# Scores and the state's output part on 64-row halves of the TensorE array, the new state on 64-column halves

## The chip, the cores and the metric

The kernel runs on one core of a Trainium2 chip. The metric is the device time of one execution in microseconds (us); less is better. Three runs of the kernel before the change took 210.63, 210.71 and 213.97 us, with a median of 210.71 us.

Times below are in us unless marked ns. TensorE is shown as two rows in the profile: PE is the stream of matmuls, PEld the stream of weight loads (each matmul multiplies a moving operand with a stationary one, which its weight load has put into the 128x128 array). DVE is VectorE, ACT is ScalarE, POOL is GpSimd, and SP issues most of the transfers.

## The reference

Two parts are computed one after the other: a gated linear attention (4 batches, 8 heads, 768 steps, head size 48), and a two-layer feed-forward over its output (3072 tokens, 384 to 2048 to 384).

```python
f = 1.0 / (1.0 + np.exp(-f_logit))
for t in range(S):
    state = f[:, :, t, :, None] * state + np.einsum('bhd,bhe->bhde', k[:, :, t], v[:, :, t])
    y[:, :, t] = np.einsum('bhd,bhde->bhe', q[:, :, t], state)
...
h = x @ w_in
g = np.maximum(0.01 * h, h)
return (g @ w_out).astype(np.float32)
```

The state of one head is a 48x48 matrix. Inputs and output are float32.

## The kernel before

**Units.** The 768 steps of a batch are cut into 6 chunks of 128 steps. A unit is one chunk of one batch with its 8 heads, and there are 24 units, ordered by chunk first and batch second (units 0 to 3 are chunk 0 of the four batches). All work of a unit is done on tiles with 128 steps or 128 channels on the partitions, in bf16 with float32 sums.

**Within a unit.** `gate_act` and `gate_pe` turn the gate's logits into logarithms and sum them over the steps with a triangular matrix (`cs`, L117, and its totals per channel, L120). `decay_act` makes the decay factors with the exponential. `scale_pool` multiplies k and q with them on POOL into `kh` and `qh`. These have 64 columns for each head, 48 of them used and the rest zero, so that a pair of heads fills 128 columns. `turn_pe` transposes the four pairs of `kh` and `qh` (L149): now a pair of heads stands on 128 partitions, the first head on partitions 0 to 63, the second on 64 to 127. `turn_dve` copies the result from PSUM to SBUF: `kT` in one copy (L155), and q in two copies (L157, L158) into the block-diagonal tile `qbd`, which has a 128-column block for each head of the pair, with zeros where the other head's partitions are.

`score_pe` then takes `kT` of a pair as the stationary operand and the two blocks of `qbd` as the moving one: one matmul with 256 columns gives the scores of both heads (L168, 4 matmuls in a unit, two PSUM banks `pw`, each with two pairs). `mask_dve` multiplies each bank with the triangle (L175). `mix_pe` gathers the unit's output `py` in one bank: the state's part with `qbd` as the stationary operand and the old state as the moving one (L187, 8 matmuls with 48 columns, not in chunk 0), and the part within the chunk with the masked scores (L191, 8 matmuls with 48 columns). `y_act` copies `py` to SBUF (L226, 384 elements on each partition). `state_pe` forms the new part of the state for a pair of heads in one matmul with 96 columns (L203, 4 matmuls, not in the last chunk); of its 128x96 result only the two diagonal blocks are used, and `state_dve` adds them with one instruction for each half of the partitions (L213, L214). `state_pool` applies the decay and makes the bf16 copy of the state (L221, L222). `x_pe` and `x_dve` transpose the output for the feed-forward.

**The feed-forward of a unit.** `up` does a quarter of the first layer (12 matmuls with 128 columns, L250, then one activation, L252), `down` half of the second (8 matmuls with 384 columns, L259), `put` copies the result out of PSUM (L264) and stores it.

**Order.** The schedule is written out by hand, and each engine works through its instructions in the order of the program. Iteration i of the main loop does the feed-forward of unit i and, between its parts, the attention of unit i+1 and the gates of units i+2 and i+3. On TensorE the order in an iteration is: transposes (`turn_pe`), two `up`, scores, gate sums, two `up`, `mix_pe`, `state_pe`, half of `down`, `x_pe`, half of `down`.

**PSUM.** Pool `ps_w` has two banks and holds only the scores. Pool `ps_s` has two banks with the tag "sm" and holds `cs`, `py`, `pt` and `px` in turn. The feed-forward's `pm` has two banks, its output one, the transposes one.

Of the kernel before, what the change touches and what calls it, by code (L numbers as in the profile page):

```python
# [9 lines left out]
FP32 = mybir.dt.float32  # L10
BF16 = mybir.dt.bfloat16
# [4 lines left out]
def kernel(  # L16
# [10 lines left out]
    nc = tc.nc  # L27

    B, H, S, D = q.shape
# [3 lines left out]
    P2 = H // 2  # L33
    KD, FF = moe_w_in.shape
# [6 lines left out]
    const = ctx.enter_context(tc.tile_pool(name="const", bufs=1))  # L41
    inp = ctx.enter_context(tc.tile_pool(name="inp", bufs=6))
    work = ctx.enter_context(tc.tile_pool(name="work", bufs=3))
# [6 lines left out]
    ps_w = ctx.enter_context(tc.tile_pool(name="ps_w", bufs=2, space=bass.MemoryType.PSUM))  # L50
    ps_s = ctx.enter_context(tc.tile_pool(name="ps_s", bufs=2, space=bass.MemoryType.PSUM))
# [5 lines left out]
    ut = const.tile([128, 128], BF16, tag="ut")  # L57
# [10 lines left out]
    lfs = [const.tile([128, H, 64], BF16, name=f"lf{i}", tag=f"lf{i}") for i in range(3)]  # L68
    qhs = [const.tile([128, H, 64], BF16, name=f"qh{i}", tag=f"qh{i}") for i in range(3)]
    khs = [const.tile([128, H, 64], BF16, name=f"kh{i}", tag=f"kh{i}") for i in range(3)]  # L70
    qbds = [const.tile([128, P2, 2, 128], BF16, name=f"qbd{i}", tag=f"qbd{i}") for i in range(2)]
    state_f = [const.tile([128, P2, D], FP32, name=f"sf{b}", tag=f"sf{b}") for b in range(B)]
    state_b = [const.tile([128, P2, D], BF16, name=f"sb{b}", tag=f"sb{b}") for b in range(B)]
    for t in lfs + qhs + khs + qbds:
        nc.vector.memset(t, 0.0)
    for t in state_f:
        nc.vector.memset(t, 0.0)
# [25 lines left out]
    st = {}  # L103
# [48 lines left out]
    def turn_dve(u):  # L152
        tp = st[u].pop("tp")
        kT = work.tile([128, P2, 128], BF16, name="kT", tag="kT")
        nc.vector.tensor_copy(out=kT, in_=tp[:, 0])  # L155
        qbd = qbds[u % 2]
        nc.vector.tensor_copy(out=qbd[0:64, :, 0, :], in_=tp[0:64, 1])  # L157
        nc.vector.tensor_copy(out=qbd[64:128, :, 1, :], in_=tp[64:128, 1])  # L158
        st[u]["kT"] = kT

    def score_pe(u):
        kT, qbd = st[u].pop("kT"), qbds[u % 2]
        st[u]["pw"] = []
        for g in range(2):
            pw = ps_w.tile([128, 4, 128], FP32, name="pw", tag="pw")
            for i in range(2):
                p = 2 * g + i
                nc.tensor.matmul(pw[:, 2 * i:2 * i + 2, :], kT[:, p, :], qbd[:, p, :, :], start=True, stop=True)  # L168
            st[u]["pw"].append(pw)

    def mask_dve(u):
        st[u]["wm"] = []
        for pw in st[u].pop("pw"):
            wm = work.tile([128, 4, 128], BF16, name="wm", tag="wm", bufs=6)
            nc.vector.tensor_mul(wm, pw, ut[:, None, :].to_broadcast([128, 4, 128]))  # L175
            st[u]["wm"].append(wm)

    def mix_pe(u):
        c, b = units[u]
        s = st[u]  # L180
        qbd, v_b, wms = qbds[u % 2], s["v"], s.pop("wm")
        py = ps_s.tile([128, 512], FP32, name="py", tag="sm")
        n = H if c == 0 else 2 * H
        i = 0
        if c > 0:
            for h in range(H):
                nc.tensor.matmul(py[:, h * D:(h + 1) * D], qbd[:, h // 2, h % 2, :], state_b[b][:, h // 2, :],  # L187
                                 start=(i == 0), stop=(i == n - 1))
                i += 1
        for h in range(H):  # L190
            nc.tensor.matmul(py[:, h * D:(h + 1) * D], wms[h // 4][:, h % 4, :], v_b[:, h, :],  # L191
                             start=(i == 0), stop=(i == n - 1))
            i += 1
        s["py"] = py

    def state_pe(u):
        c, b = units[u]
        if c == NCH - 1:
            return
        kh, v_b = khs[u % 3], st[u]["v"]  # L200
        pt = ps_s.tile([128, P2, 2 * D], FP32, name="pt", tag="sm")
        for p in range(P2):
            nc.tensor.matmul(pt[:, p, :], kh[:, 2 * p:2 * p + 2, :], v_b[:, 2 * p:2 * p + 2, :],  # L203
                             start=True, stop=True)
        st[u]["pt"] = pt

    def state_dve(u):
        c, b = units[u]
        if c == NCH - 1:
            return  # L210
        pt = st[u].pop("pt")
        sf = state_f[b]
        nc.vector.tensor_add(sf[0:64], sf[0:64], pt[0:64, :, 0:D])  # L213
        nc.vector.tensor_add(sf[64:128], sf[64:128], pt[64:128, :, D:2 * D])  # L214

    def state_pool(u):
        c, b = units[u]
# [5 lines left out]

    def y_act(u):
        xn = work.tile([128, KD], BF16, name="xn", tag="xn")
        nc.scalar.copy(out=xn, in_=st[u].pop("py")[:, 0:KD])  # L226
        st[u]["xn"] = xn

    def x_pe(u):
# [57 lines left out]
    gate_act(2)  # L287
    turn_pe(0)
    turn_dve(0)
    score_pe(0)  # L290
    mask_dve(0)
    mix_pe(0)
    state_pe(0)
    y_act(0)
    state_dve(0)
    state_pool(0)
    x_pe(0)
    x_dve(0)

    for i in range(NU):  # L300
# [3 lines left out]
        if n1 < NU:  # L304
            turn_pe(n1)
            turn_dve(n1)
        up(i, 0)
        up(i, 1)
        if n1 < NU:
            score_pe(n1)  # L310
            mask_dve(n1)
# [6 lines left out]
        if n1 < NU:  # L318
            mix_pe(n1)
            y_act(n1)  # L320
            state_pe(n1)
            state_dve(n1)
            state_pool(n1)
# [38 lines left out]
```

## Time and profile before

| what | value |
|---|---|
| median of three runs | 210.71 us |
| span of the profiled execution | 209.4 us |
| PE busy | 177.8 us (85%), 2432 matmuls |
| PEld busy | 146.1 us (70%), 2432 weight loads |
| ACT busy | 108.7 us (52%) |
| DVE busy | 97.4 us (46%) |
| POOL busy | 76.8 us (37%) |
| granted TensorE clock | 1.000 |

The span runs from the first instruction to the last; the profile lists no other time for this execution, so its own time is taken as the span and the 1.3 us by which the median stands above it. A group of the profile has a line number, an engine, what is written from what, the shape, and the mean duration of one instruction. For a matmul the group also names the part of the array it runs on; before the change this is 128*128 everywhere. A matmul's duration holds its way through the array, which overlaps with the next matmuls, so the pace of a row of matmuls is read from their starts and not from their durations.

From 41.69 us on the main loop is regular. An iteration takes 7.10 us where the next unit is in chunk 0, and 7.30 us from chunk 1 on (63.20 to 70.50, 128.92 to 136.22 and others). In an iteration of 7.30 us DVE is busy for 3.99 us, ACT for 4.47 us and POOL for 3.09 us, while PE has no gap that the profile shows.

### The profile page before, as it was taken

Reading aid. Unit: us, or ns where it says so; the run is one execution under the profiler, and the core shown is the slowest. Engines: PE = TensorE matmul, PEld = TensorE weight load, DVE = VectorE, ACT = ScalarE, POOL = GpSimd, SP = SyncE. Lnnn points to the kernel's source line nnn. Section 1 sums busy time; section 2 is a strip of 40 time slices with the busy share of each in tenths; the row PEclk is TensorE's granted clock in tenths of the full one; section 3 lists DMA queues with packets and bytes.
Section 4 is the critical chain, followed back from the end, with each engine's and each line's share of the span. In section 5 each row is a group of like instructions: output and inputs, shape, how many; then the busy total and the mean of one; then the engine's idle time right before and its main releaser. Section 6 shows DMA issues by size and latency. Waiting matters only on the chain.

```text
span 209.4 us, 5831 instructions
## 1 busy us (share of the span) xinstructions
PE 177.8 (85%) x2432; PEld 146.1 (70%) x2432; DVE 97.4 (46%) x223; ACT 108.7 (52%) x237; POOL 76.8 (37%) x129
## 2 busy tenths in 40 slices
PE   0000149999999999999999999999999999999993
PEld 0000028788779788877988887798888778877881
DVE  8000044466546545654654565465455545633511
ACT  4000332775576458447645845774585567555540
POOL 8300071542553255145325524532552454034000
PEclk9999999999999999999999999999999999999999
DMA  6999999998796479568647846956695681100111
GB/s 114 171 195 184 199 191 189 156 219 163 121 176 143 105 136 177 114 118 163 147 102 133 186 111 116 157 116 141 128 187 113 119 153 41 38 28 18 38 41 38
DMA packets 106267, 27.12 MB, mean 130 GB/s; under 512 B 100352, under 2 KB 105472, under 8 KB 106240
## 3 DMA queue, kind: packets, MB, share of 16 engines
q1 hardware_dynamic: 103296, 23.60, 59.5%
q0 software_dynamic: 2944, 3.15, 9.0%
q8 instruction: 19, 0.31, 0.6%
q14 instruction: 8, 0.07, 0.1%
HBM read 25.17 MB, written 4.72 MB: 143 GB/s over the span
## 4 chain that ended last, share of the span: by engine, by line
PE 83%; issue 10%; POOL 4%; DVE 1%; ACT 0%; POOLq 0%
PE pm L250 32%; PE pm L259 30%; PE pw L168 6%; PE tp L149 5%; PE py L191 2%; PE px L233 2%; PE py L187 2%; PE cs L117 2%; PE pt L203 2%; POOL w_in_b L94 2%; POOL w_out_b L99 1%; POOL kh L139 1%; PE cs L120 1%; DVE wm L175 1%; POOL qh L140 1%
## 5 line engine op out<-in xcount | busy, mean ns | idle before, releaser
L252 ACT ACTIVATE gT<-pm 128x512 bf16<-128x512 f32 x96 | 56.2, 601 | 64.1 <-PE pm L250 62.3
L250 PE MATMUL pm<-xT,w_in_b 128*128 128x128 bf16 x1152 | 73.4, 221 | 0.0
L259 PE MATMUL pm<-w_out_b,gT 128*128 128x384 bf16 x384 | 70.1, 326 | 0.0
L250 PEld LDWEIGHTS <-w_in_b 128*128 128x128 bf16 x1152 | 67.2, 99 | 0.6
L139 POOL TENSOR_TENSOR kh<-k_raw,em_t 128x384 bf16<-128x384 f32 x24 | 22.0, 916 | 110.5 <-ACT em_t L129 105.7
L259 PEld LDWEIGHTS <-gT 128*128 128x128 bf16 x384 | 35.2, 98 | 18.8
L175 DVE TENSOR_TENSOR wm<-pw,ut 128x512 bf16<-128x512 f32 x48 | 30.9, 686 | 12.7 <-PE pw L168 11.9
L117 PE MATMUL cs<-lf,ut 128*128 128x384 bf16 x24 | 8.1, 339 | 24.9 <-ACT lf L111 24.9
L264 DVE COPY osb<-pm 128x384 f32<-128x384 f32 x24 | 13.4, 558 | 26.6 <-PE pm L259 26.6
L109 ACT ACTIVATE e_t<-f_raw 128x384 f32<-128x384 f32 x24 | 12.9, 536 | 23.7 <-DMA f_raw<-in_f_logit_dram 23.7
L120 PEld LDWEIGHTS <-lf 128*128 128x128 bf16 x80 | 5.0, 99 | 25.2 <-issue 23.8
L140 POOL TENSOR_TENSOR qh<-q_raw,a_t 128x384 bf16<-128x384 f32 x24 | 21.9, 914 | 0.0
L155 DVE COPY kT<-tp 128x512 bf16<-128x512 bf16 x24 | 10.0, 415 | 23.6 <-PE tp L149 23.6
L238 DVE COPY xT<-px 128x384 bf16<-128x384 bf16 x24 | 8.6, 358 | 22.2 <-PE px L233 22.2
L213 DVE TENSOR_TENSOR sf<-sf,pt 64x192 f32<-64x192 f32 x20 | 6.9, 346 | 22.2 <-PE pt L203 22.2
L168 PE MATMUL pw<-qbd,kT 128*128 128x256 bf16 x96 | 14.8, 277 | 1.3 <-DVE qbd L158 1.3
L129 ACT ACTIVATE em_t<-cs 128x384 bf16<-128x384 f32 x24 | 11.8, 491 | 4.5 <-PE cs L120 3.7
L111 ACT ACTIVATE lf<-e_t 128x384 bf16<-128x384 f32 x24 | 12.5, 523 | 0.8
L168 PEld LDWEIGHTS <-kT 128*128 128x128 bf16 x96 | 9.4, 99 | 4.3 <-DVE kT L155 0.8
L226 ACT CAST xn<-py 128x384 bf16<-128x384 f32 x24 | 11.4, 474 | 1.5 <-PE py L191 1.5
L142 POOL CAST v_b<-v_raw 128x384 bf16<-128x384 f32 x24 | 12.1, 505 | 0.0
L130 ACT ACTIVATE a_t<-cs 128x384 bf16<-128x384 f32 x24 | 11.6, 485 | 0.0
(37 smaller groups left out, 155.3 us busy)
## 6 DMA issues: line engine op xcount, KB each, us to landing
f_raw<-in_f_logit_dram SPq DMA_DIRECT2D x24, 192.0 KB, 3.2
k_raw<-in_k_dram SPq DMA_DIRECT2D x24, 192.0 KB, 3.8
q_raw<-in_q_dram SPq DMA_DIRECT2D x24, 192.0 KB, 4.0
v_raw<-in_v_dram SPq DMA_DIRECT2D x24, 192.0 KB, 4.3
out_dram<-osb SPq DMA_DIRECT2D x24, 192.0 KB, 2.0
w_in_b<-in_moe_w_in_dram POOLq DMA_DIRECT2D x6, 256.0 KB, 8.8
w_out_b<-in_moe_w_out_dram POOLq DMA_DIRECT2D x2, 768.0 KB, 18.2
```

The lines of the kernel that those rows point to most:

```text
L109: nc.scalar.activation(e, f, AF.Exp, scale=-1.0)
L111: nc.scalar.activation(lf[:, :, 0:D], e, AF.Ln, bias=1.0)
L117: nc.tensor.matmul(cs[:, 0:H * D], ut, lf[:, :, 0:D], start=True, stop=True)
L139: nc.gpsimd.tensor_mul(khs[u % 3][:, :, 0:D], r["k"], st[u]["em"])
L140: nc.gpsimd.tensor_mul(qhs[u % 3][:, :, 0:D], r["q"], st[u]["a"])
L142: nc.gpsimd.tensor_copy(out=v_b, in_=r["v"])
L168: nc.tensor.matmul(pw[:, 2 * i:2 * i + 2, :], kT[:, p, :], qbd[:, p, :, :], start=True, stop=True)
L175: nc.vector.tensor_mul(wm, pw, ut[:, None, :].to_broadcast([128, 4, 128]))
L250: nc.tensor.matmul(pm[:, i, :], w_in_b[:, kk, ff * 128:(ff + 1) * 128], s["xT"][:, kk, :], start=(kk == 0), stop=(kk == NK - 1))
L252: nc.scalar.activation(s["g"][:, 4 * g:4 * g + 4, :], pm, AF.Prelu, alpha=0.01)
L259: nc.tensor.matmul(s["pm2"], s["g"][:, ff, :], w_out_b[:, ff, :], start=(ff == 0), stop=(ff == NF - 1))
L264: nc.vector.tensor_copy(out=osb, in_=st[u]["pm2"])
```

## The change

The block-diagonal `qbd` goes. q is copied from PSUM in one piece into `qT`, in the same layout as `kT`. A score matmul now takes one head: 48 partitions of one half (0 to 47 or 64 to 111), so that it uses 64 rows of the array and 128 columns, with 128 moving columns; the two heads of a pair are issued one after the other, on the two row halves, and write to different banks. The state's part of y is split over row halves in the same way, its 8 matmuls keeping 48 moving columns. Heads of even number gather in one PSUM bank and those of odd number in another; the two output tiles `py` now come from pool `ps_w`, whose two banks they share in turn with the scores. `y_act` becomes two copies of 192 elements with a strided output. The new state is made one head at a time: 128 rows and 64 columns of the array, 48 moving columns, 8 matmuls where there were 4, and the result lies compactly, so that one addition replaces two.

```diff
-    qbds = [const.tile([128, P2, 2, 128], BF16, name=f"qbd{i}", tag=f"qbd{i}") for i in range(2)]
...
-    for t in lfs + qhs + khs + qbds:
+    for t in lfs + qhs + khs:
         nc.vector.memset(t, 0.0)
...
         nc.vector.tensor_copy(out=kT, in_=tp[:, 0])
-        qbd = qbds[u % 2]
-        nc.vector.tensor_copy(out=qbd[0:64, :, 0, :], in_=tp[0:64, 1])
-        nc.vector.tensor_copy(out=qbd[64:128, :, 1, :], in_=tp[64:128, 1])
-        st[u]["kT"] = kT
+        qT = work.tile([128, P2, 128], BF16, name="qT", tag="qT")
+        nc.vector.tensor_copy(out=qT, in_=tp[:, 1])
+        st[u]["kT"], st[u]["qT"] = kT, qT
 
     def score_pe(u):
-        kT, qbd = st[u].pop("kT"), qbds[u % 2]
-        st[u]["pw"] = []
-        for g in range(2):
-            pw = ps_w.tile([128, 4, 128], FP32, name="pw", tag="pw")
-            for i in range(2):
-                p = 2 * g + i
-                nc.tensor.matmul(pw[:, 2 * i:2 * i + 2, :], kT[:, p, :], qbd[:, p, :, :], start=True, stop=True)
-            st[u]["pw"].append(pw)
+        kT, qT = st[u].pop("kT"), st[u]["qT"]
+        pws = [ps_w.tile([128, P2, 128], FP32, name="pw", tag="pw") for j in range(2)]
+        for p in range(P2):
+            for j in range(2):
+                rows = slice(64 * j, 64 * j + D)
+                nc.tensor.matmul(pws[j][:, p, :], kT[rows, p, :], qT[rows, p, :], start=True, stop=True)
+        st[u]["pw"] = pws
...
     def mix_pe(u):
         c, b = units[u]
         s = st[u]
-        qbd, v_b, wms = qbds[u % 2], s["v"], s.pop("wm")
-        py = ps_s.tile([128, 512], FP32, name="py", tag="sm")
-        n = H if c == 0 else 2 * H
-        i = 0
+        qT, v_b, wms = s.pop("qT"), s["v"], s.pop("wm")
+        pys = [ps_w.tile([128, P2, D], FP32, name="py", tag="pw") for j in range(2)]
         if c > 0:
-            for h in range(H):
-                nc.tensor.matmul(py[:, h * D:(h + 1) * D], qbd[:, h // 2, h % 2, :], state_b[b][:, h // 2, :],
-                                 start=(i == 0), stop=(i == n - 1))
-                i += 1
-        for h in range(H):
-            nc.tensor.matmul(py[:, h * D:(h + 1) * D], wms[h // 4][:, h % 4, :], v_b[:, h, :],
-                             start=(i == 0), stop=(i == n - 1))
-            i += 1
-        s["py"] = py
+            for p in range(P2):
+                for j in range(2):
+                    rows = slice(64 * j, 64 * j + D)
+                    nc.tensor.matmul(pys[j][:, p, :], qT[rows, p, :], state_b[b][rows, p, :],
+                                     start=(p == 0), stop=False)
+        for j in range(2):
+            for p in range(P2):
+                nc.tensor.matmul(pys[j][:, p, :], wms[j][:, p, :], v_b[:, 2 * p + j, :],
+                                 start=(c == 0 and p == 0), stop=(p == P2 - 1))
+        s["py"] = pys
 
     def state_pe(u):
...
-        pt = ps_s.tile([128, P2, 2 * D], FP32, name="pt", tag="sm")
+        pt = ps_s.tile([128, P2, D], FP32, name="pt", tag="sm")
         for p in range(P2):
-            nc.tensor.matmul(pt[:, p, :], kh[:, 2 * p:2 * p + 2, :], v_b[:, 2 * p:2 * p + 2, :],
-                             start=True, stop=True)
+            for j in range(2):
+                nc.tensor.matmul(pt[64 * j:64 * j + 64, p, :], kh[:, 2 * p + j, :], v_b[:, 2 * p + j, :],
+                                 start=True, stop=True)
...
-        nc.vector.tensor_add(sf[0:64], sf[0:64], pt[0:64, :, 0:D])
-        nc.vector.tensor_add(sf[64:128], sf[64:128], pt[64:128, :, D:2 * D])
+        nc.vector.tensor_add(sf, sf, pt)
...
     def y_act(u):
         xn = work.tile([128, KD], BF16, name="xn", tag="xn")
-        nc.scalar.copy(out=xn, in_=st[u].pop("py")[:, 0:KD])
+        xv = xn.rearrange("t (p j d) -> t j p d", p=P2, j=2)
+        for j, py in enumerate(st[u].pop("py")):
+            nc.scalar.copy(out=xv[:, j], in_=py)
```

`mask_dve` keeps its two instructions of 128x512 in shape; a bank now holds four heads of the same parity.

More of the change, by code (lines that the diff above doesn't have):

```diff
@@ L173, in mask_dve @@
         for pw in st[u].pop("pw"):
-            wm = work.tile([128, 4, 128], BF16, name="wm", tag="wm", bufs=6)
-            nc.vector.tensor_mul(wm, pw, ut[:, None, :].to_broadcast([128, 4, 128]))
+            wm = work.tile([128, P2, 128], BF16, name="wm", tag="wm", bufs=6)
+            nc.vector.tensor_mul(wm, pw, ut[:, None, :].to_broadcast([128, P2, 128]))
             st[u]["wm"].append(wm)
```

## Prediction

> **What bounds the kernel now.** I read the page's busy shares first, then the chain that ended last, then that chain piece by piece through one iteration, then the instructions in order of time around the pieces that change.
>
> ```profile
> PE 177.8 (85%) x2432; PEld 146.1 (70%) x2432; DVE 97.4 (46%) x223; ACT 108.7 (52%) x237; POOL 76.8 (37%) x129
> PE 83%; issue 10%; POOL 4%; DVE 1%; ACT 0%; POOLq 0%
> ```
>
> TensorE holds 83% of the chain, and no other engine is busy for much over half of the span. So an edit counts by the TensorE time it takes or gives in an iteration; DVE, ACT and POOL count only if they come too late for TensorE. One iteration of the chain (start, duration, piece):
>
> ```profile
> 128.92 0.45 PE tp L149 x8
> 129.37 1.34 PE pm L250 x24
> 130.71 0.57 PE pw L168 x4
> 131.28 0.16 PE cs L117
> 131.44 0.08 PE cs L120 x4
> 131.52 1.36 PE pm L250 x24
> 132.88 0.20 PE py L187 x8
> 133.08 0.20 PE py L191 x8
> 133.28 0.17 PE pt L203 x4
> 133.45 1.30 PE pm L259 x8
> 134.75 0.17 PE px L233 x3
> 134.92 1.30 PE pm L259 x8
> ```
>
> These pieces fill the 7.30 us to the next transposes at 136.22, so there is nothing to gain but in them. The change touches pw (0.57), py L187 (0.20) and pt (0.17): 0.94 of 7.30 us, 13%. The rest can only be disturbed. The instructions of the same iteration show that pw is not all work. On TensorE:
>
> ```profile
> 129.20 1.50 PE L250 MATMUL pm<-xT,w_in_b 128*128 128x128 bf16 x24
> 130.68 0.60 PE L168 MATMUL pw<-qbd,kT 128*128 128x256 bf16 x4
> 131.11 0.33 PE L117 MATMUL cs<-lf,ut 128*128 128x384 bf16 x1
> ...
> 132.72 0.36 PE L187 MATMUL py<-sb,qbd 128*128 128x48 bf16 x8
> ```
>
> and, on DVE,
>
> ```profile
> 130.20 0.43 DVE L158 COPY qbd<-tp 64x512 bf16<-64x512 bf16 x1
> 131.09 1.29 DVE L175 TENSOR_TENSOR wm<-pw,ut 128x512 bf16<-128x512 f32 x2 [0.47 <-PE pw L168]
> ```
>
> The 24 matmuls from 129.20 go at 1.34/24 = 0.056 each and have streamed in by 130.54; pw starts at 130.68, just after the last copy of q ends (130.63). So TensorE waits 0.14 for DVE, and the scores themselves take 131.11 - 130.68 = 0.43. The waits view books no such wait, because the modelled ends of the matmuls cover it.
>
> **Part 1, turn_dve: the wait goes.** Two copies into qbd (406 and 428 ns) become one of 128x512, like kT's (415 ns). q is ready 0.4 earlier, at about 130.2, before the 24 matmuls are through (130.54). The 0.14 goes in 23 iterations: -3.2 us. Next late are the matmuls themselves. DVE's other savings (0.35 for one state addition, the first memsets) lie beside TensorE's work and give nothing; if DVE were late they would be worth themselves.
>
> **Part 2, scores.** 4 matmuls of 256 columns (0.43) become 8 of 128. If the two halves of the array work side by side, four pairs at the 0.056 of 128 columns take 0.22: -0.21 x 24 = -5.0 us. If they go one after the other, 8 x 0.056 = 0.45: nothing. I take the first: the halves share no rows, and the banks differ.
>
> **Part 3, the state's part of y.** 8 matmuls with 48 columns remain 8, each with its weight load. The trace's pace for such a pair is 0.20/8 = 0.025 (L187), and L191 with the same shape has it too. Moving columns alone would need 48/128 x 0.056 = 0.021, so the pace is close to what one stream needs; side by side it could halve (-0.10 x 20 = -2.0 us). I take 0, by the row: nothing in the trace goes below 0.020 per matmul (L120, 0.08/4, with a single column).
>
> **Part 4, the new state.** 4 matmuls of 96 columns (0.17) become 8 of 48. At L187's pace that is 0.20, +0.03. If each weight load ran uncovered at its duration of 98 ns (L203's load row), 8 x 0.098 = 0.78, +0.61; if pairs of column halves overlapped fully, half of 0.20, -0.07. I take +0.03 x 20 = +0.6 us; the ends are -1.4 and +12.2. [...]
>
> **Part 5, switches of the array's form: the unknown.** Every matmul of the trace runs as 128*128. After the change TensorE goes to 64-row halves and back for the scores, again for the state's part of y, and to 64-column halves and back for the new state. Chunk 0 has 4 switches in a unit (no state's part), chunks 1 to 4 have 6, chunk 5 has 4 (no new state): 4x4 + 16x6 + 4x4 = 128. No row shows one. Lower end: 0, a switch is as free as going from one weight to the next (I exclude a gain, nothing is saved by it). Upper end: the matmuls before must be finished, and the next weight load starts only then: the tail of a matmul, plus a load.
>
> ```profile
> L120 PE MATMUL cs<-ones_col,lf 128*128 128x1 bf16 x80 | 4.9, 165 | 0.0
> L120 PEld LDWEIGHTS <-lf 128*128 128x128 bf16 x80 | 5.0, 99 | 25.2 <-issue 23.8
> ```
>
> A matmul with one column lasts 165 ns, so this is the tail; with a load of 99 ns it is 264 ns. The ends are far apart: 128 x 0 = 0 and 128 x 0.264 = 33.8 us. I take the tail alone, 128 x 0.165 = 21.1 us: halves must not meet results of the whole array on their way out, and the tail is the trace's row for how long such results are under way, whereas loads here go ahead of their matmuls (PEld starts L168's at 130.49, 0.19 before). [...]
>
> **Part 6, new waits and ACT.** py now lies in the scores' banks, so the first state matmul waits until the masks have read them; queued behind it on TensorE are L191, pt and down, the whole rest of the iteration. Before, the masks end at 131.09 + 1.29 = 132.38, 0.34 ahead of L187 at 132.72. After, without switches, the way from the scores' start to L187 is 0.22 + 0.16 + 0.08 + 1.36 = 1.82; both banks are full only after the last pair (start at 0.19, lasting 0.22: 0.41) and the masks end at 0.41 + 1.29 = 1.70 plus a few hundredths. Margin about 0.1, and each switch between widens it: cost 0; if the margin went to -0.1, +2 us. The copy of y: 128x384 takes 474 ns and 128x4 takes 181 ns (L226, L133), so 192 elements take about 327 and two copies 0.65, +0.18. They end at 133.41 + 0.65 = 134.06, still 0.37 before the loads of L233 begin at 134.43: cost 0, up to +0.18 x 24 = 4 without the first half of down as cover. ps_s holds one tile less in a unit, so nothing there comes later. No DMA is moved; the inputs are loaded five units ahead.
>
> **Start.** In unit 0 the scores wait from 28.79 (kT) to 29.58 for the q copies; one copy less brings them 0.4 earlier, and the longer copy of y takes 0.18 back: -0.2.
>
> **The sum,** on the span of 209.4: -3.2 - 5.0 + 0 + 0.6 + 21.1 + 0 - 0.2 = +13.3, so 222.7. The median of the three runs is 1.3 above the span: **224.0 us, 6% slower**. A difference of 2% (4.2 us) is about what a measurement of this kernel can tell from no change.
>
> **Rivals.** Break-even is where 128 switches eat 7.8 us: 0.061 each.
> 1. Switches are free and the halves overlap: -7.8 on the span, 201.6, with the bounds of parts 3, 4 and 6 200 to 204; the time is **203** us. For it: nothing in the trace shows that form matters, weight loads already go ahead, and even switching between transposes and matmuls costs nothing (8 transposes, 0.45, at the full 0.056). Against: the transposes keep the array's form. It decides below 0.027 a switch (128 x 0.027 = 3.5, so -2%).
> 2. Only the array empties while the next operands are already fetched, say one matmul's 0.056: +7.2, span 208.8, time **210**, within 2% from 0.027 to 0.094. [...]
> 3. Loads wait too (0.264), and those of the 64-column halves run bare in part: 33.8 - 7.8 is +26 (time 237), up to **248** with part 4's upper end. For it: the loads' own 99 ns; against: loads run ahead everywhere here.
> 4. The change doesn't do what it says, the halves take turns: forecast + 5.0, **229**.
>
> **Chances.** Forecast (0.094 to 0.2 a switch, 215 to 228) 0.38; rival 1 0.25; rival 2 0.22; rival 3 0.10; rival 4 0.05. Faster by over 2%: 0.25. Within 2%: 0.22. Slower: 0.53. The range must leave out no more than 0.2: low 202.5, which leaves out about a third of rival 1 (0.08), and high 234, which leaves out most of rival 3 (0.09). As both signs hold much, the forecast's own range is 215 to 228.
>
> **What would show it.** Forms 64*128 and 128*64 in the matmul groups; gaps of 0.1 to 0.2 between the last start before a switch (plus its streaming) and the first after, six in an iteration; an iteration from 128.9 on of about 7.30 - 0.14 - 0.21 + 0.03 + 6 x 0.165 = 7.97 instead of 7.30; score starts in close pairs, 0.22 from first to following work; pt at 0.20; L158's like and its wait gone. The prediction is wrong if switches cost under 0.09, if scores take 0.45, or if DVE's masks become the wait ahead of the state matmuls.

## The result and the profile after

The changed kernel takes 214.87 us against 211.78 us before (medians of 20 runs each). The ratio, taken here and below without the runs that lie over 1.5% above the fastest of their kernel, is 1.0115 with a 95% interval of 1.0074 to 1.0157. So it is slower by 1.2%, clear of the runs' scatter, but by less than the 2% that the prediction took as about the least that can be told from no change. The profiled execution took 213.17 us with a span of 211.4, so 1.8 us lie around the span (the forecast had taken 1.3).

The page of the changed kernel, busy shares and the chain's shares by engine:

```profile
PE 180.3 (85%) x2608; PEld 143.0 (68%) x2608; DVE 79.4 (38%) x177; ACT 110.2 (52%) x261; POOL 76.1 (36%) x129
PE 84%; SPq 11%; DMA 3%; ACT 1%; issue 0%; DVE 0%
```

TensorE still sets the end. DVE lost 18 us of work, and nothing came of it, as it was not what TensorE waited for beyond the 0.14 of the q copies. (The 11% on SP's queue are the wait for the first inputs, which the page of before booked under other names.)

The chain of the changed kernel through one iteration (start, duration, piece):

```profile
130.13 0.45 PE tp L148 x8
130.58 1.34 PE pm L248 x24
131.92 0.33 PE pw L165 x8
132.25 0.27 PE cs L116
132.52 0.08 PE cs L119 x4
132.60 1.36 PE pm L248 x24
133.96 0.20 PE py L184 x8
134.16 0.30 PE py L188 x8
134.47 0.24 PE pt L200 x8
134.71 1.41 PE pm L257 x8
136.11 0.17 PE px L231 x3
136.28 1.30 PE pm L257 x8
137.58 0.45 PE tp L148 x8
```

An iteration of chunks 1 to 4 takes 7.45 instead of 7.30. The scores went from 0.57 to 0.33. But each piece that follows a change of form is longer by about a tenth, though its own work is unchanged: cs 0.16 to 0.27, the masked scores' part of y 0.20 to 0.30, the first half of down 1.30 to 1.41. py L184 stayed at 0.20 and pt went from 0.17 to 0.24.

The groups of the changed kernel name the forms (busy us, mean ns of one):

```profile
L165 PE MATMUL pw<-qT,kT 48*128 48x128 bf16 x192 | 10.0, 226 | 0.8 <-DVE qT L156 0.8
...
L200 PE MATMUL pt<-v_b,kh 128*64 128x48 bf16 x160 | 6.3, 197 | 0.0
...
L184 PE MATMUL py<-sb,qT 48*128 48x48 bf16 x160 | 5.4, 183 | 0.0
```

The starts of single matmuls in the trace tell work and change of form apart (medians over the loop, ns). "First to last" is from the first to the last start of a piece, "into" from the last start of the piece before to the first start of this one; for the same form, "into" is the spacing that the piece before has anyway (56 after 128 columns, 25 after 48).

| piece | into, before | into, after | first to last, before | first to last, after |
|---|---|---|---|---|
| scores | 193 | 151 | 325 | 182 |
| gate sums | 109 | 148 | | |
| state's part of y | 56 | 151 | 179 | 93 |
| masked scores' part of y | 25 | 111 | 176 | 190 |
| new state | 26 | 112 | 125 | 119 |
| first half of down | 41 | 122 | 1138 | 1149 |

Each of the six changes of form costs 86 to 97 ns beyond the usual spacing. (Into down, 25 ns is the usual spacing behind the 48 columns that the new state's matmuls have after the change; the 41 of the table stands behind 96 columns.) Coming back to the whole array costs another 11 to 14 ns between the first and the second matmul (cs to its totals 173 instead of 162; 190 instead of 176 in the masked part; 1149 instead of 1138 in down). That is about 0.098 a change, 0.59 in an iteration. Against it stand 0.137 for the wait that went, 0.20 for the scores, 0.09 for the state's part of y and 0.02 for the new state. The difference, 0.15, is what the iteration grew by. Going into a half form also delays the second pair (the second pair of scores starts 67 ns after the first, the later pairs 56 after the one before); this is counted in the length of the piece itself.

One change of form in order of time, the last `up` matmul and the scores on TensorE, then the scores' weight loads:

```profile
131.70 0.22 PE L248 MATMUL pm<-xT,w_in_b 128*128 128x128 bf16 x1
131.85 0.40 PE L165 MATMUL pw<-qT,kT 48*128 48x128 bf16 x8
```

```profile
131.85 0.23 PEld L165 LDWEIGHTS <-kT 48*128 48x128 bf16 x8
```

And the masks on DVE, which have to end before the state's part of y can start on TensorE:

```profile
132.28 1.29 DVE L172 TENSOR_TENSOR wm<-pw,ut 128x512 bf16<-128x512 f32 x2 [0.89 <-PE pw L165]
```

```profile
133.89 0.27 PE L184 MATMUL py<-sb,qT 48*128 48x48 bf16 x8
```

**How the runs are compared below.** The loop can start only when the second unit's gate logits have landed, and that moment differs between executions, whatever the kernel: the activation that waits for them starts at 24.35 us in the profile of before, at 23.77 in that of the changed kernel, and between 24.05 and 27.83 in the experiments. These 4 us are nearly as much as the total times of the kernel before range over (209.41 to 214.37 us), so this may be much of their scatter; in runs without a profile the moment is not known. So for each run I give the ratio of the times, and, from its trace, the iteration of chunks 1 to 4 and the time from that activation to the end, which leaves this wait out. For the two kernels these are 7.30 and 7.45, and 185.06 and 187.60: +2.5 us. The last column still holds the first two units, which take different times too: from the activation to the third unit's transposes it is 17.18 us before, 17.47 in the changed kernel, and 16.29 (direct) to 17.73 (wait_alone) elsewhere. From these transposes to the end the changed kernel is at +2.3 us, direct at +0.6, turns at +2.5 and grouped at -5.1. So the iteration is the surest of the three figures.

| run | iteration | from the second logits to the end | against before |
|---|---|---|---|
| before | 7.30 | 185.06 | |
| after | 7.45 | 187.60 | +2.5 |
| cols_alone | 7.47 | 188.08 | +3.0 |
| scores_alone | 7.19 | 182.73 | -2.3 |
| y_alone | 7.43 | 187.43 | +2.4 |
| copies_alone | 7.32 | 185.48 | +0.4 |
| no_cols | 7.27 | 184.29 | -0.8 |
| direct | 7.34 | 184.78 | -0.3 |
| mix_split | 7.65 | 191.43 | +6.4 |
| turns | 7.46 | 186.99 | +1.9 |
| one_half | 7.67 | 192.63 | +7.6 |
| wait_alone | 7.51 | 190.74 | +5.7 |
| grouped | 7.06 | 179.62 | -5.4 |

### The profile page after: what moved, and what is told of

The parts are those of the page before. It is cut to its first block, busy times and chain, and to the rows that moved or that the text cites. A ratio compares the mean times of both kernels' runs of the same rounds, so it can differ in the third digit from the quotient of the medians.

```text
span 211.4 us, 6228 instructions
## 1 busy us (share of the span) xinstructions
PE 180.3 (85%) x2608; PEld 143.0 (68%) x2608; DVE 79.4 (38%) x177; ACT 110.2 (52%) x261; POOL 76.1 (36%) x129
## 4 chain that ended last, share of the span: by engine, by line
PE 84%; SPq 11%; DMA 3%; ACT 1%; issue 0%; DVE 0%
PE pm L248 31%; PE pm L257 30%; SPq L86 11%; PE tp L148 5%; PE pw L165 4%; PE py L188 3%; PE cs L116 3%; DMA f_raw<-in_f_logit_dram 3%; PE pt L200 2%; PE px L231 2%; PE py L184 2%; PE cs L119 1%; DVE osb L262 0%; ACT xn L224 0%; ACT e_t L108 0%
## 5 line engine op out<-in xcount | busy, mean ns | idle before, releaser
L257 PEld LDWEIGHTS <-gT 128*128 128x128 bf16 x384 | 34.7, 98 | 19.5
L210 DVE TENSOR_TENSOR sf<-sf,pt 128x192 f32<-128x192 f32 x20 | 7.1, 354 | 23.7 <-PE pt L200 23.7
L224 ACT CAST xn<-py 128x192 bf16<-128x192 f32 x48 | 13.0, 326 | 0.4 <-PE py L188 0.4
L110 ACT ACTIVATE lf<-e_t 128x384 bf16<-128x384 f32 x24 | 12.5, 523 | 0.8
L217 POOL TENSOR_TENSOR sf<-sf,a_end 128x192 f32<-128x192 f32 x20 | 10.2, 511 | 2.4 <-DVE sf L210 2.4
L165 PE MATMUL pw<-qT,kT 48*128 48x128 bf16 x192 | 10.0, 226 | 0.8 <-DVE qT L156 0.8
```

The costliest lines, as they stand in the source:

```text
L165: nc.tensor.matmul(pws[j][:, p, :], kT[rows, p, :], qT[rows, p, :], start=True, stop=True)
L224: nc.scalar.copy(out=xv[:, j], in_=py)
L257: nc.tensor.matmul(s["pm2"], s["g"][:, ff, :], w_out_b[:, ff, :], start=(ff == 0), stop=(ff == NF - 1))
```

## The experiments

The theory after the result: each change of the array's form costs about a tenth of a microsecond (0.098 by the table), the pairs on two halves do run side by side (182 ns for the scores instead of 325), and the wait for q is gone; the sum of the three is the result. The rivals: the loss lies in the half-size matmuls themselves, or in y's shared banks and double copy.

### Each part of the change alone

**cols_alone**: the new state on column halves in the kernel before.

```diff
-        pt = ps_s.tile([128, P2, 2 * D], FP32, name="pt", tag="sm")
+        pt = ps_s.tile([128, P2, D], FP32, name="pt", tag="sm")
...
-            nc.tensor.matmul(pt[:, p, :], kh[:, 2 * p:2 * p + 2, :], v_b[:, 2 * p:2 * p + 2, :],
+            for j in range(2):
+                nc.tensor.matmul(pt[64 * j:64 * j + 64, p, :], kh[:, 2 * p + j, :], v_b[:, 2 * p + j, :],
...
-        nc.vector.tensor_add(sf[0:64], sf[0:64], pt[0:64, :, 0:D])
-        nc.vector.tensor_add(sf[64:128], sf[64:128], pt[64:128, :, D:2 * D])
+        nc.vector.tensor_add(sf, sf, pt)
```

> The kernel before, with the new state alone on 64-column halves (8 matmuls, one addition). Theory (each change of the array's form costs 0.09 to 0.10 beyond the usual spacing, and two changes are all that counts here): an iteration of chunks 1 to 4 goes from 7.30 to 7.46, 20 units make +3.2 us. Rival (the recorded forecast's 0.165 for a change): 7.63, +6.6 us. Rival (the loads of 64 columns run uncovered): the 8 matmuls take over 0.4, above 7.6.

Measured: iteration 7.47, +3.0 us, ratio 1.0121 (1.0075 to 1.0166). The chain of this kernel:

```profile
138.16 0.20 PE py L191 x8
138.36 0.24 PE pt L204 x8
138.60 1.41 PE pm L259 x8
```

The new state (0.17 before) and the half of down behind it (1.30 before) are 0.18 longer together. The eight matmuls themselves take 119 ns from first to last start, against 125 for the four before: their loads are not bare. Splitting the new state brings 0.02 on TensorE at most and costs two changes of form.

**scores_alone**: the scores on row halves in the kernel before, with q still in the block-diagonal tile.

```diff
-                nc.tensor.matmul(pw[:, 2 * i:2 * i + 2, :], kT[:, p, :], qbd[:, p, :, :], start=True, stop=True)
...
+                rows = slice(64 * j, 64 * j + D)
+                nc.tensor.matmul(pws[j][:, p, :], kT[rows, p, :], qbd[rows, p, j, :], start=True, stop=True)
```

> The kernel before, with the scores alone on 64-row halves; q is still copied in two pieces into the block-diagonal tile, and each score matmul reads its head's block of it. Theory (the change of form ahead of the scores runs beside the wait of 0.14 for the second copy of q, and only the change back is paid): the way from the last up matmul to the first score stays 0.193, the scores and the change back take 0.33 instead of 0.43: iteration 7.21, about -2.2 us. Rival (wait and change of form add up): 7.30, no difference.

Measured: iteration 7.19, -2.3 us, ratio 0.9799 (0.9706 to 0.9892). Its chain:

```profile
138.06 0.36 PE pw L167 x8
138.42 0.27 PE cs L117
```

The first score starts 152 ns after the last up matmul, not 193 as expected: it needs only the first half of q. In one iteration the copy of the second half ends at 137.99; the second score starts at 138.041, 0.05 after it, as a score that waits for a copy does in wait_alone below, and the first at 137.997, too early to have waited for it. First to last start take 207 ns instead of 182. So the change of form and the wait run beside each other, a little more than I had thought. Scores alone pay, because half of their price falls into the wait.

**y_alone** and **copies_alone**: y in two banks of the scores' pool with two copies by ACT; in the first kernel the state's part runs on row halves, in the second on the whole array. In y_alone:

```diff
-        py = ps_s.tile([128, 512], FP32, name="py", tag="sm")
+        pys = [ps_w.tile([128, P2, D], FP32, name="py", tag="pw") for j in range(2)]
...
+                    rows = slice(64 * j, 64 * j + D)
+                    nc.tensor.matmul(pys[j][:, p, :], qbd[rows, p, j, :], state_b[b][rows, p, :],
```

In copies_alone the last two lines are instead:

```diff
+                    nc.tensor.matmul(pys[j][:, p, :], qbd[:, p, j, :], state_b[b][:, p, :],
```

> The kernel before, with the state's part of y alone on 64-row halves, in two banks of the scores' pool, and with two copies by ACT. Theory (two changes of form at 0.09 to 0.10, less 0.086 because the pairs run side by side): iteration 7.41, about +2.2 us. Rival (the gain of the pairs pays for the changes): 7.30, 0. Rival (the shared banks and the copies cost too): above 7.45.

> The kernel before, with y in two banks of the scores' pool and copied by ACT in two pieces, but every matmul on the whole array as before. Theory (the shared banks and the longer copy are covered): iteration 7.30, 0 within 0.5 us. Rival (the new wait for the masks or the later copy of y holds up TensorE): above 7.35, over +1 us.

Measured: y_alone 7.43, +2.4 us, ratio 1.0053 (0.9986 to 1.0120); copies_alone 7.32, +0.4 us, ratio 0.9920 (0.9869 to 0.9971). The shared banks and the two copies cost 0.02 in an iteration, and this sits in the scores (first to last start 338 instead of 325), not at y. The two kernels differ by 0.11 in an iteration, which is the two changes of form (0.20) less what the pairs give (0.087). That the total time of copies_alone came out 0.8% lower has no counterpart in its loop; I know no reason for it. The three pieces in the chain of y_alone, of which the second comes back to the whole array:

```profile
136.84 0.20 PE py L187 x8
137.05 0.30 PE py L192 x8
137.35 0.17 PE pt L203 x4
```

**no_cols**: the changed kernel with the new state on the whole array (this part of the change undone).

> The changed kernel, with the new state on the whole array as before. Theory (two changes of form fewer in 20 units): iteration 7.29 instead of 7.45, -3.2 us against the changed kernel, about -1 us against the kernel before. Rival (the changed kernel's loss lies in y's shared banks): 7.45 stays.

Measured: iteration 7.27, -3.3 us against the changed kernel, ratio to before 0.9985 (0.9952 to 1.0019). Without the new state's part the kernel is level with the one before: what the scores win and what the state's part of y costs (-0.11 and +0.13 in an iteration, each alone) about cancel, and the new state's 0.17 is the loss that is left.

### Is it the change of form?

**direct**: the same matmuls as in the changed kernel, in another order: the new state, on column halves, directly behind the state's part of y, on row halves. One return to the whole array is saved.

```diff
             for p in range(P2):
                 for j in range(2):
...
+        state_pe(u)
         for j in range(2):
             for p in range(P2):
                 nc.tensor.matmul(pys[j][:, p, :], wms[j][:, p, :], v_b[:, 2 * p + j, :],
...
             y_act(n1)
-            state_pe(n1)
```

> The changed kernel, with the new state's matmuls moved between the state's part of y (64-row halves) and the masked scores' part (whole array): the same matmuls, one change of form fewer in chunks 1 to 4, if going from row halves to column halves costs as one change. Theory (the cost belongs to each change of form): iteration 7.35 instead of 7.45, 16 units make -1.6 us. Rival (the cost belongs to the half-size matmuls themselves, whose loads cannot go ahead): 7.45, no difference.

**mix_split**: the same matmuls again, y in two parts of two pairs each, so that there are two changes more.

```diff
+        for part in ((0, 1), (2, 3)):
             if c > 0:
-                for p in range(P2):
+                for p in part:
...
             for j in range(2):
-                for p in range(P2):
+                for p in part:
```

> The changed kernel, with y gathered in two parts: state's part and masked scores' part of pairs 0 and 1, then of pairs 2 and 3. The same matmuls with two more changes of form in 20 units. Theory (0.09 to 0.10 for a change): iteration 7.64 to 7.67 instead of 7.45, about +4 us against the changed kernel. Rival (the cost does not belong to the change): 7.45.

Measured: direct 7.34 (-0.11 against the changed kernel; ratio to before 1.0027, 0.9981 to 1.0073), mix_split 7.65 (+0.20; ratio to before 1.0295, 1.0238 to 1.0351). By the table these are -2.8 and +3.8 us against the changed kernel; of direct's -2.8, 1.2 lie ahead of the third unit, and 1.6 in the rest, as the theory has it. The chain of direct, then that of mix_split:

```profile
134.77 0.20 PE py L184 x8
134.97 0.24 PE pt L201 x8
135.21 0.30 PE py L189 x8
135.51 1.30 PE pm L258 x8
```

```profile
138.94 0.15 PE py L185 x4
139.09 0.20 PE py L189 x4
139.29 0.15 PE py L185 x4
139.45 0.20 PE py L189 x4
139.65 0.24 PE pt L201 x8
```

In direct the half of down is back at 1.30, since it follows work of its own form, and from row halves to column halves costs about the same as any change (109 ns into the new state where 25 would be usual). In mix_split each group of four pays what the group of eight paid before. With the same matmuls, one change fewer gives a tenth, two more cost two tenths: the cost belongs to the change and not to the half-size matmul.

### Do the halves work side by side?

**turns**: the four scores of the upper half first, then the four of the lower.

```diff
-        for p in range(P2):
-            for j in range(2):
+        for j in range(2):
+            for p in range(P2):
```

> The changed kernel, with the four score matmuls of the upper row half first and then the four of the lower half, instead of in pairs. Theory (pairs run side by side only when neighbours in the order are on different halves): the first to the last score start grows from 0.182 to about 0.35 to 0.40, iteration 7.62 to 7.67, +4 to +5 us against the changed kernel. Rival (the halves do not overlap in any case, and scores of 48 rows are short for another reason): 7.45 stays.

Measured: 191 ns from first to last start, iteration 7.46, ratio 1.0112 (1.0053 to 1.0170). My expectation fell, and two readings were left: the halves overlap although the program has them in turns, or a matmul on half of the rows is simply faster. **one_half** tells them apart.

```diff
-                rows = slice(64 * j, 64 * j + D)
+                rows = slice(0, D)
```

> The changed kernel, with both heads' score matmuls on the upper 64 rows (it computes the even head's scores twice and leaves the odd head's out): the same eight matmuls of 48 rows and 128 columns, on one half of the array. Theory (each half takes its own matmuls one after the other at 0.056, and the halves work side by side whatever the order): first to last start 7 x 0.056 = 0.39 instead of 0.18, iteration 7.66. Rival (a matmul on half of the rows simply streams faster, 0.03 for 128 columns): 0.18 and 7.45 stay.

Measured, in one run (220.67 us against 213.21 of the kernel before beside it): 402 ns from first to last start, iteration 7.67. The scores in the chain of turns, then of one_half:

```profile
139.39 0.34 PE pw L165 x8
```

```profile
129.56 0.55 PE pw L165 x8
```

On one half the starts stand 56 ns apart (67 for the first two), the pace of 128 columns on the whole array. So the halves do work side by side. In turns the second start comes 14 ns after the first, closer than any two starts on one half (56 in one_half): the lower half's first matmul started ahead of three matmuls that stand before it in the program. The semaphores in the trace of turns say the same: the second start is one that waits, as the program's first matmul into a bank does, and the last two starts are those that report a bank as done, though the program has these as its fourth and its eighth matmul. So across the halves the matmuls of this run did not start in the order of the program.

### The wait for q

**wait_alone** was meant to take the wait away with nothing else changed, by giving the second piece of q to ACT.

```diff
-        nc.vector.tensor_copy(out=qbd[64:128, :, 1, :], in_=tp[64:128, 1])
+        nc.scalar.copy(out=qbd[64:128, :, 1, :], in_=tp[64:128, 1])
```

> The kernel before, with the second piece of q copied by ACT instead of DVE, so that the scores need not wait, and every matmul as before. Theory (the wait of 0.14 in 23 iterations was real, though the waits view does not book it): iteration 7.16, -3.2 us. Rival (it was a pause of TensorE between forms of matmul and not a wait): 7.30, 0.

Measured: iteration 7.51, +5.7 us, ratio 1.0316 (1.0245 to 1.0387). It made the wait longer instead. The instructions in order of time, ACT and then TensorE:

```profile
128.22 0.58 ACT L158 COPY qbd<-tp 64x512 bf16<-64x512 bf16 x1 [2.67 <-DVE qbd L157]
...
128.85 0.60 PE L168 MATMUL pw<-qbd,kT 128*128 128x256 bf16 x4 [0.18 <-ACT qbd L158]
```

ACT's copy starts only behind DVE's (at 128.22; DVE's ends at 128.14) and takes 581 ns instead of 428, and the scores start 0.05 after it ends. From the last up matmul to the first score it is 403 ns instead of 193, and the iteration grew by the same 0.21. So the wait was real, and its length is what the q copies make it. The view books 0.18 of it (and nothing in the kernel before), because the last up matmul is 0.22 long in the profile, with a modelled end, which covers the first part: 0.403 less 0.22 is the 0.18. The removal alone was not tried in a cleaner way; in the changed kernel the way into the scores is 151 ns, the same as into the state's part of y, ahead of which the masks had ended 0.32 before.

### A version that keeps the gain

**grouped**: the changed kernel with the new state on the whole array, and the state's part of y directly behind the scores, in the same form. Two changes of form in an iteration are left of six.

```diff
         score_pe(n1)
+        read_pe(n1)
...
+    def read_pe(u):
+        c, b = units[u]
+        s = st[u]
+        qT = s.pop("qT")
+        s["py"] = pys = [ps_s.tile([128, P2, D], FP32, name="py", tag="sm") for j in range(2)]
+        if c > 0:
+            for p in range(P2):
+                for j in range(2):
+                    rows = slice(64 * j, 64 * j + D)
+                    nc.tensor.matmul(pys[j][:, p, :], qT[rows, p, :], state_b[b][rows, p, :],
+                                     start=(p == 0), stop=False)
...
-        cs = ps_s.tile([128, 512], FP32, name="cs", tag="sm")
+        cs = ps_t.tile([128, 512], FP32, name="cs", tag="tp")
...
-        pt = ps_s.tile([128, P2, 2 * D], FP32, name="pt", tag="sm")
+        pt = ps_w.tile([128, P2, 2 * D], FP32, name="pt", tag="pw")
...
-        px = ps_s.tile([128, NK, 128], BF16, name="px", tag="sm")
+        px = ps_w.tile([128, NK, 128], BF16, name="px", tag="pw")
```

> The changed kernel, with the new state on the whole array, and the state's part of y issued right after the scores, in the same form (its two banks now come from the pool of the small tiles; the gate sums share the transposes' bank, the new state and the transposed output share the scores' banks). Two changes of form in an iteration instead of six. Theory: iteration 7.09, about -5.0 us against the kernel before (ratio 0.976). Rival (the banks' new order brings a wait, for instance the gate sums behind the copies of q and k): 7.2 or more, at most -2.3 us.

Measured: iteration 7.06, -5.4 us from the second logits to the end, ratio 0.9823 (0.9757 to 0.9888), 208.97 us against 212.55 of the kernel before beside it. Its chain:

```profile
131.16 0.33 PE pw L165 x8
131.50 0.10 PE py L184 x8
131.59 0.27 PE cs L116
131.86 0.08 PE cs L119 x4
131.94 1.36 PE pm L252 x24
133.30 0.20 PE py L193 x8
133.50 0.17 PE pt L203 x4
```

The state's part of y is now 0.10, half of what it was, and the pieces that follow are at their old lengths but for the gate sums. It is faster than both kernels, 1.8% faster than the one before.

## Why the prediction was wrong

The forecast was 224.0 us and 6% slower; measured were 214.87 us and 1.2% slower, about a fifth of that. The range (202.5 to 234) holds the time. The direction and the cause (the changes of form outweigh the rest) were right; the size of the main term was not. The measured price of a change, 0.098, lies at the border of two of the prediction's cases, just inside the forecast's 0.094 to 0.2 and just above rival 2's upper bound of 0.094; the time, 214.87, lies just under the forecast's own 215 to 228. None of the three signs of being wrong that the prediction names came true, but the first (under 0.09 a change) only just.

- **Part 5, the changes of form, is the step that failed.** I took the whole tail of a matmul, 0.165, by the row of the one-column matmul, assuming that the halves must not meet the results of the whole array on their way out; no run shows such a condition. Measured is about 0.098: 128 x 0.098 = 12.5 us instead of 21.1, which is 8.6 of the 11 us between the forecast's +13.3 and what the traces show. In one iteration the first matmul of the new form starts at 131.853, while the last one of the old form (start 131.700, 0.220 long) ends at 131.920 by the profile: the new form starts 0.067 before that. As these ends are modelled, it stays open whether the results are really out by then. The price is 0.067 under the tail of 0.165, so a part of the tail is not paid, as rival 2 had it, but it is more than the 0.056 that rival 2 took; what the 0.165 consists of, no run shows. What I said of loads held for the kernel before only: there the first load of each piece in the table starts 23 to 192 ns ahead of its matmul, 1 to 2 ns after the matmul before it has started; at the six changes it starts at most 5 ns ahead (here at 131.848). So this lead is lost, and the matmul does not wait for the load's end in the profile, 93 ns after its start. How much of the 0.098 is the late load and how much a wait for the matmuls of the old form, no run separates. Where the time is lost, direct, mix_split and the pairs agree on: 84 to 97 ns at each change of form, while neighbours on two halves, which keep the form, start 4 ns apart.
- **Part 1** held: the wait of 0.137 is gone.
- **Part 2** held: -0.21 was said; with the change of form taken out the scores went from 0.434 to 0.238, -0.20.
- **Part 3** failed in the cautious direction: I took 0, by the pace of one stream, though I had named the halving as the bound. 93 ns instead of 179, -1.7 us in 20 units. Two starts fall 4 ns apart. The floor of 0.020 that I read from L120 in the chain is not in its starts, which stand 25 to 28 ns apart, and it is one of a single stream.
- **Part 4**: +0.03 was said; without the changes around it the new state is shorter by some 0.02. The bound of bare loads is ruled out: a load of 64 columns lasts 112 ns in the profile, but eight matmuls start within 119.
- **Part 6** held. The masks end at 132.28 + 1.29 = 133.57, 0.32 ahead of the first state matmul at 133.89, and copies_alone shows 0.02 for banks and copies.

With the measured sizes the sum is -3.2 - 4.7 - 1.7 - 0.4 + 12.5 = +2.5. The traces show +2.0 on the span, +2.5 from the second unit's logits on and +2.3 from the third unit's transposes on. The -0.2 that the forecast has for the start is left out: no run shows it, and the start varies by more than that from kernel to kernel. That the time came out so close to 215 is chance: parts 3 and 4 gave 2.7 us more than was said, while in the runs beside the result the kernel before itself took 211.78 us, 1.1 more than the forecast started from.

## What to carry to other kernels

In these runs halves of the array paid only by the run of work done in one form: 7.06 us an iteration with two changes of form (grouped) against 7.45 with six and 7.30 with none. So count the changes of form in the loop first, measure the price of one (0.098 us here), and put the pieces of one form next to each other before splitting anything. Neither piece of about 0.2 us earned two changes by itself: the state's part of y alone made the iteration 0.13 longer, the new state alone 0.17. The scores, at 0.43, just covered theirs (0.20 won, 0.20 paid) and won where one change fell into a wait (7.19 in scores_alone); the state's part of y won as soon as it stood next to them (0.10 instead of 0.20 in grouped). And the wait of 0.137 that ended just ahead of the scores was hidden by the modelled end of the matmul before, 0.22 after its start: look at the starts.

## What was not expected

- The two row halves were served independently of the order in turns: eight score matmuls that the program has four and four start in pairs 14 ns apart (191 ns from first to last, against 402 when all are on one half, in one_half).
- The price of a change hardly depended on the direction or on what ran before: 84 to 97 ns between the starts beyond the usual spacing, after 128-column, 48-column, row-half and column-half matmuls alike, and from row halves to column halves it is paid once (84 ns).
- Short matmuls in pairs went below the 25 ns of one stream: eight with 48 columns started within 82 to 93 ns on row halves and within 119 ns on column halves.
- When the second unit's logits land moves by up to 4 us between executions, though all these kernels load their inputs alike (23.77 to 27.83 us), more than the change itself moves the time.
